# Pack attention and FFN on one core: the first batch's second softmax by halves of the tokens, two loads from ScalarE's queue, one subtraction on GpSimd, and new steps

## The chip, the cores and the metric

The program runs on 1 core of one Trainium2 chip. The metric is the device time in microseconds. Several executions were timed; one more was recorded by the hardware profiler, and all lines called profile come from it. In the lines PE is TensorE, PEld its weight loads, DVE is VectorE, ACT is ScalarE, POOL is GpSimd, and SP is the engine whose queue starts most transfers.

## The reference

Two attention stages with few "pack" tokens, then a feed-forward network. Per batch (8) and head (8): 576 tokens, head dimension 64, 32 pack tokens.

```python
def sm_attn(qq, kk, vv):
    s = scale * np.matmul(qq, kk.transpose(0, 1, 3, 2))
    s = s - np.max(s, axis=-1, keepdims=True)
    a = np.exp(s)
    a = a / (np.sum(a, axis=-1, keepdims=True) + 1e-09)
    return np.matmul(a, vv)
p_packed = sm_attn(p, k, v)          # first softmax: over 576 tokens
out = sm_attn(q, p_packed, p_packed) # second softmax: over 32 pack tokens
...                                  # heads side by side: x is 4608 x 512
h = x @ w_in                         # 512 x 2048
g = np.maximum(h, 0.0) + alpha * np.minimum(h, 0.0)
return g @ w_out                     # 2048 x 512
```

The weights w_in and w_out come as 64-bit floats and are turned into 32-bit ones on the chip.

## The kernel before

**Attention** is a Python generator, `attention(b, tp, exact)`, one for each batch and each half of its heads (tp 0 or 1: four heads, as two pairs). Between two `yield`s it issues one step: loads of K, the scores of the pack tokens (`scores`), their softmax, the transposed weights `aT` (L328, L332), the packed values (`pack`, L345 and L355, then L373), then the scores of all tokens against the packed keys and the **second softmax**. That one is laid out by 32-wide groups: a transpose of 32x32 blocks (L422 or L427, to `t`), a maximum of each group of 32 (L429, `m`), a subtraction (L431), an exponential on ScalarE (L433), a sum (L435, `z`), EPS added (L436), a reciprocal (L437), a product (L438), and a transpose back (L443, to `a_f`, in batch 0). Batches 0 and 1 use plain 32-bit matmuls (`exact`); the others split every operand in a high and a low part, so that `split_x`, `split_v` and `split_pw` have ScalarE cast the high part and VectorE or GpSimd subtract it (L180, L309, L455, L613). The low part of p, `s`, is such a subtraction (L256), done twice for each of the batches 2 to 7. For batch 0 the matmuls' scores stay in PSUM.

**The packed weights.** The packed values are multiplied into w_in first (`pw`), so that one FFN unit is `second softmax weights x pw`. `convert` makes a 32-bit tile of w_in or w_out from a 64-bit one (`wraw`): ScalarE makes `mag` and `low` (L121, L123), VectorE does L125, L128, L132 and L137 or L139, and for a split tile L141 and L142. Until it is needed for w_out, the space of the tiles of w_out holds raw tiles; `SPARE` says how many of them serve raw w_in tiles in turn. `packed_w_fine` (L525) and `packed_w_first` (L485) make pw for batch 0 from columns of w_in; `packed_w` (L595 to L597, copied out by L600) serves the other batches, from fresh, whole or split tiles. The split tiles are kept in DRAM (`w_split`) and loaded again (L567) for the batches 2 to 7.

**FFN units.** `first(k, f)` is a unit: the 288 tokens of half batch k by 128 of the 2048 hidden columns (`ps_h`: L625 in batch 0, L637 to L639 later), then the leaky ReLU: `neg` on ScalarE (L643), L644 on VectorE, the high part `gh` on ScalarE (L649), the low part `gl` on VectorE (L650). `second(k, f)` multiplies it by w_out into four accumulators (`acc`: L667 to L669), two units later (`AHEAD = 2`). A batch's columns are taken in sweeps, and the accumulators of a part are kept in `part`. At the end of a half batch four tiles `ot` go to DRAM (`outT`, L685).

**What sets the order.** Up to the first unit a string, `zzzAzzzzzPzzzoPzzzzozzzP`, says which generator takes its next step: z both attentions of batch 0, the second three steps behind the first, P `packed_w_fine`, o a w_out tile, A alpha. After that a list `plan` of (first unit, generator, pace) does: pace 1 is a step at each unit, 3 one at every third, -3 three at each. The numbers in it are `WO` (w_out: start, how many at once, then how many units apart), `AT1` (attention of batch 1), `PW1` (packed_w of batch 1 alone), `PW01` and `PW01B` (packed_w of batches 0 and 1), `A2` (attention of batches 2 and 3, their packed_w) and `AG` (the same for each later pair of batches). From the program so written, the framework's scheduler sets the order on each engine, by its own estimate of times, and places the semaphore waits. Each engine then takes its instructions strictly in order, and so does each engine's queue of transfers.

Of the kernel before, what the change touches and what calls it, by code (L numbers as in the profile page):

```python
# [28 lines left out]
def pack_attention_ffn_kernel(  # L29
# [199 lines left out]
    def attention(b, tp, exact=False):  # L229
# [11 lines left out]
        split = (lambda x: x) if exact else split_x  # L241
        if tp == 0:
            praw = sm.tile([P, NP, N], F32, name="praw", tag="praw", bufs=1)
            nc.sync.dma_start(out=praw, in_=pT[b])
        k0 = load_x(kT, b, pr0)
        k1 = load_x(kT, b, pr1)
        yield
        if tp == 0:
            for r in range(2):
                rs, cs = slice(r * 64, r * 64 + 64), slice(r * N, r * N + N)  # L250
                if exact:
                    for i in range(2):
                        nc.scalar.copy(out=s1f[rs, i::2, i, cs], in_=praw[rs, i::2])
                else:
                    nc.scalar.copy(out=s1[rs, :, 0, cs], in_=praw[rs])
                    nc.vector.tensor_tensor(  # L256
                        out=s1[rs, :, 1, cs], in0=praw[rs], in1=fv(s1[rs, :, 0, cs]),
                        op=ALU.subtract,
                    )
# [160 lines left out]
        if b == 0:  # L420
            for hf in range(2):
                nc.vector.transpose(  # L422
                    out=t1.rearrange("p g n -> p (g n)")[:, hf * HS : hf * HS + HS],
                    in_=s2[hf][:, :HS],
                )
# [3 lines left out]
        nc.vector.tensor_reduce(out=m2, in_=t1, axis=AX.X, op=ALU.max)  # L429
# [7 lines left out]
        nc.vector.reciprocal(out=z2, in_=z2)  # L437
        eng.tensor_tensor(out=t1, in0=t1, in1=z2.broadcast_to([P, NG, 32]), op=ALU.mult)  # L438
        yield
        if b < XF:  # L440
            if b not in result:
                result[b] = at.tile([P, 2, S], F32, name="a_f", tag="a_h")
            nc.vector.transpose(  # L443
                out=result[b][:, tp, :], in_=t1.rearrange("p g n -> p (g n)")
            )
            done.add(("a", b, tp))
            yield
            split_pt()
            return
# [4 lines left out]
        nc.scalar.copy(out=a_h[:, tp, :], in_=s2)
        nc.gpsimd.tensor_tensor(out=a_l[:, tp, :], in0=s2, in1=fv(a_h[:, tp, :]), op=ALU.subtract)  # L455
# [159 lines left out]

    def first(k, f):
        tok = slice((k % 2) * HS, (k % 2) * HS + HS)
        assert all(("a", k // 2, tp) in done for tp in range(2)), ("a", k)
        assert k < 2 and ("wf", f) in done or all(("w", k // 2, f // 4, pr) in done for pr in range(4)), ("w", k, f)
        ps = ps_h.tile([P, 512], F32, name="ps_h", tag="h")  # L620
        if k < 2 * XF:
            th, a_f = pw[k // 2, f // 4], result[k // 2]
            fs = slice((f % 4) * P, (f % 4) * P + P)
            for i in range(2):
                nc.tensor.matmul(  # L625
                    ps[:, :HS], th[:, i, fs], a_f[:, i, tok], start=(i == 0), stop=(i == 1)
                )
        else:
            a_h, a_l = result[k // 2]
            key = (k, f // 2)  # L630
            if key not in pj:
                split_pw(*key)
            th, tl = pj[key]
            fs = slice((f % 2) * P, (f % 2) * P + P)
            for i in range(2):
                hi, lo = (i == 0), (i == 1)
                nc.tensor.matmul(ps[:, :HS], th[:, i, fs], a_h[:, i, tok], start=hi, stop=False)  # L637
                nc.tensor.matmul(ps[:, :HS], th[:, i, fs], a_l[:, i, tok], start=False, stop=False)  # L638
                nc.tensor.matmul(ps[:, :HS], tl[:, i, fs], a_h[:, i, tok], start=False, stop=lo)  # L639
# [9 lines left out]
        nc.scalar.copy(out=gh, in_=x)  # L649
        nc.vector.tensor_tensor(out=gl, in0=x, in1=fv(gh), op=ALU.subtract)  # L650
        gs[k, f] = (gh, gl)
# [75 lines left out]

    def zipped(*gens):
        gens = list(gens)
        while gens:  # L730
            for x in list(gens):
                try:
                    next(x)
                except StopIteration:
                    gens.remove(x)
            yield

    def load_alpha():
        nc.sync.dma_start(out=al, in_=alpha)
        nc.vector.tensor_scalar(  # L740
            out=nal, in0=al, scalar1=-1.0, scalar2=1.0, op0=ALU.mult, op1=ALU.add
        )
        yield
# [5 lines left out]
    z = zipped(attention(0, 0, True), after(3, attention(0, 1, True)))  # L749
# [2 lines left out]
    la = load_alpha()

    for ch in "zzzAzzzzzPzzzoPzzzzozzzP":
        next({"z": z, "P": wf, "o": wo, "A": la}[ch], None)
# [3 lines left out]
    WO, W1, AT1 = (-7, 5, 4), 0, (-2, 2, -3)
    PW1, PW01, PW01B = (7, -2), (13, 3), (25, -8)  # L760
    A2 = (24, 29, 34, 38, 52)
    AG = (0, 4, 10, 17, 27)
# [58 lines left out]
```

## Time and profile before

| | |
|---|---|
| times of 3 runs | 806.47, 807.29 (median), 808.75 us |
| the profiled execution | 805.65 us |
| its span, first to last instruction | 803.9 us |
| mean granted TensorE clock | 0.991 of full speed |
| busy: TensorE, VectorE, ScalarE, GpSimd | 769.7, 500.7, 544.9, 305.6 us |
| moved by transfers | 93.79 MB |

The profiled execution's own time is 1.75 us above its span; that lies around the span. Most questions are asked of a stretch: which engine has no gap in it, and for whom TensorE waits. In rows of the timeline the first two numbers are start and duration in us, x the number of instructions merged in the row, and the bracket is the idle time of that engine before the row, with the instruction that ended it.

### The profile page before, as it was taken

The numbers are of one execution on the slowest core, as the hardware profiler recorded it, in microseconds if no ns is written. First come the engines' busy times: TensorE is split into PE (matmuls) and PEld (weight loads), VectorE is DVE, ScalarE is ACT, GpSimd is POOL, SyncE is SP. The second block draws the span as 40 slices with busy tenths as digits, with TensorE's granted clock in tenths as the row PEclk, the third lists the DMA queues.
The fourth block names the chain that finished last, engine by engine and source line by source line (L and its number), as shares of the span: only waits on it lengthen the run. The fifth ranks groups of instructions, "written<-read, shape, count | busy, mean of one in ns | idle before, by whom it ended". The sixth has DMA issues, their size and how long they took to land.

```text
span 803.9 us, 15166 instructions
## 1 busy us (share of the span) xinstructions
PE 769.7 (96%) x5376; PEld 729.5 (91%) x5376; DVE 500.7 (62%) x1110; ACT 544.9 (68%) x1258; POOL 305.6 (38%) x291
## 2 busy tenths in 40 slices
PE   5789999999989899999999999999999999999997
PEld 4557778989989799999999999999999999999997
DVE  4999899877877445666755265665753344444443
ACT  5787898876756877776768866776758744444443
POOL 2101311235436434666565135576443123222220
PEclk9989999999999999999999999999999999999999
DMA  9977777322223843222125722221007300000000
GB/s 299 379 246 240 254 283 255 118 67 70 89 77 94 274 162 107 84 60 89 53 71 172 240 97 61 74 60 61 1 31 228 113 30 2 30 1 31 1 31 30
DMA packets 58459, 93.79 MB, mean 117 GB/s; under 512 B 5136, under 2 KB 36880, under 8 KB 58384
## 3 DMA queue, kind: packets, MB, share of 16 engines
q1 hardware_dynamic: 58384, 92.83, 35.8%
q8 instruction: 42, 0.69, 0.3%
q14 instruction: 33, 0.27, 0.1%
HBM read 72.88 MB, written 19.92 MB: 115 GB/s over the span
## 4 chain that ended last, share of the span: by engine, by line
PE 83%; DVE 6%; ACT 3%; DMA 2%; issue 1%; SPq 0%; ACTq 0%; DVEq 0%
PE acc L667 16%; PE acc L669 16%; PE acc L668 15%; PE ps_h L637 7%; PE ps_h L638 7%; PE ps_h L639 7%; PE ps_h L625 3%; PE ps_m L350 2%; PE ps_m L595 2%; PE ps_m L216 2%; PE ps_m L597 1%; PE ps_m L596 1%; PE ps_m L217 1%; PE ps_m L328 1%; PE ps_m L212 1%
## 5 line engine op out<-in xcount | busy, mean ns | idle before, releaser
L667 PE MATMUL acc<-gh,wo 128*128 128x288 f32 x1024 | 286.1, 299 | 6.8 <-ACT gh L649 6.4
L668 PE MATMUL acc<-gh,wo 128*128 128x288 f32 x1024 | 282.6, 295 | 0.0
L644 DVE SCALAR_TENSOR_TENSOR ps_h<-neg,nal,ps_h 128x288 f32<-128x288 f32 x256 | 132.6, 518 | 146.8 <-ACT neg L643 146.1
L613 POOL TENSOR_TENSOR pwl<-pw,pwh 128x512 fp32r<-128x512 f32 x96 | 124.1, 1293 | 217.9 <-ACT pwh L611 183.2
L667 PEld LDWEIGHTS acc<-gh,wo 128*128 128x128 f32 x1024 | 192.7, 188 | 11.9 <-ACT gh L649 9.3
L669 PE MATMUL acc<-gl,wo 128*128 128x288 f32 x1024 | 201.5, 299 | 0.0
L668 PEld LDWEIGHTS acc<-gh,wo 128*128 128x128 f32 x1024 | 192.7, 188 | 1.5 <-issue 0.2
L650 DVE TENSOR_TENSOR gl<-ps_h,gh 128x288 fp32r<-128x288 f32 x256 | 116.0, 454 | 77.2 <-ACT gh L649 73.0
L669 PEld LDWEIGHTS acc<-gl,wo 128*128 128x128 f32 x1024 | 158.3, 188 | 2.8
L649 ACT CAST gh<-ps_h 128x288 fp32r<-128x288 f32 x256 | 102.0, 399 | 81.8 <-DVE ps_h L644 79.8
L637 PE MATMUL ps_h<-a_h,pwh 128*128 128x288 f32 x448 | 133.6, 298 | 3.4 <-DVE gl L650 3.4
L643 ACT ACTIVATE neg<-ps_h 128x288 f32<-128x288 f32 x256 | 104.6, 409 | 44.5 <-PE ps_h L639 33.8
L638 PE MATMUL ps_h<-a_l,pwh 128*128 128x288 f32 x448 | 132.1, 295 | 0.0
L639 PE MATMUL ps_h<-a_h,pwl 128*128 128x288 f32 x448 | 132.0, 295 | 0.0
L611 ACT CAST pwh<-pw 128x512 fp32r<-128x512 f32 x112 | 69.4, 620 | 61.9 <-PE ps_h L638 60.5
L180 POOL TENSOR_TENSOR xl<-xraw,xh 128x576 fp32r<-128x576 f32 x48 | 70.0, 1460 | 103.3 <-ACT xh L179 100.5
L637 PEld LDWEIGHTS ps_h<-a_h,pwh 128*128 128x128 f32 x448 | 84.2, 188 | 5.1 <-DVE gl L650 4.6
L638 PEld LDWEIGHTS ps_h<-a_l,pwh 128*128 128x128 f32 x448 | 84.3, 188 | 0.4
L639 PEld LDWEIGHTS ps_h<-a_h,pwl 128*128 128x128 f32 x448 | 84.1, 188 | 0.2
L600 ACT COPY pw<-ps_m 64x512 f32<-64x512 f32 x120 | 69.6, 580 | 7.2 <-PE ps_m L597 4.8
L309 POOL TENSOR_TENSOR vs<-vraw,vs 128x640 fp32r<-128x640 f32 x24 | 38.2, 1591 | 19.1 <-ACT vs L308 18.1
L219 ACT COPY lo<-ps_m 64x288 f32<-64x288 f32 x96 | 37.5, 396 | 6.5 <-PE ps_m L217 4.5
(128 smaller groups left out, 989.1 us busy)
## 6 DMA issues: line engine op xcount, KB each, us to landing
w<-w_split SPq DMA_DIRECT2D x48, 512.0 KB, 4.3
xraw<-in_kT SPq DMA_DIRECT2D x32, 288.0 KB, 2.9
xraw<-in_qT SPq DMA_DIRECT2D x32, 288.0 KB, 2.8
outT<-ot SPq DMA_DIRECT2D x64, 144.0 KB, 2.0
vraw<-in_v SPq DMA_DIRECT2D x32, 256.0 KB, 2.9
wraw<-in_w_in SPq DMA_DIRECT2D x16, 512.0 KB, 5.4
wraw<-in_w_out SPq DMA_DIRECT2D x16, 512.0 KB, 4.9
w_split<-w SPq DMA_DIRECT2D x16, 512.0 KB, 3.6
```

The lines of the kernel that those rows point to most:

```text
L180: nc.gpsimd.tensor_tensor(out=xl, in0=raw, in1=fv(xh), op=ALU.subtract)
L613: low.tensor_tensor(out=tl, in0=src, in1=fv(th), op=ALU.subtract)
L637: nc.tensor.matmul(ps[:, :HS], th[:, i, fs], a_h[:, i, tok], start=hi, stop=False)
L638: nc.tensor.matmul(ps[:, :HS], th[:, i, fs], a_l[:, i, tok], start=False, stop=False)
L639: nc.tensor.matmul(ps[:, :HS], tl[:, i, fs], a_h[:, i, tok], start=False, stop=lo)
L643: nc.scalar.activation(out=neg, in_=x, func=AF.Relu, scale=-1.0)
L644: nc.vector.scalar_tensor_tensor(out=x, in0=neg, scalar=nal[:, f : f + 1], in1=x, op0=ALU.mult, op1=ALU.add)
L649: nc.scalar.copy(out=gh, in_=x)
L650: nc.vector.tensor_tensor(out=gl, in0=x, in1=fv(gh), op=ALU.subtract)
L667: nc.tensor.matmul(acc[o][:, :HS], wo_t[f][:, 0, os_], gh, start=begin, stop=False)
L668: nc.tensor.matmul(acc[o][:, :HS], wo_t[f][:, 1, os_], gh, start=False, stop=False)
L669: nc.tensor.matmul(acc[o][:, :HS], wo_t[f][:, 0, os_], gl, start=False, stop=end)
```

## The change

1. **Second softmax of batch 0 in two halves of 288 tokens.** A generator `half(hf)` does the nine steps for 9 of the 18 groups of a partition, all of it on VectorE but the exponential. Each attention of batch 0 runs `half(0)` itself, and puts `half(1)` in the list `later`, which the plan steps twice at each unit from unit 0 on. A unit `first(k, f)` of batch 0 now needs only the half of its own 288 tokens.
2. **Loads.** p of batch 0 and alpha are issued from ScalarE's queue, alpha ahead of everything else; the first step of batch 0's attention is issued before ScalarE's first exponential.
3. **The subtraction L256** (low part of p, batches 2 to 7) goes from VectorE to GpSimd.
4. **Steps.** The string loses A and one z (`drain` takes what is left); SPARE is 4, not 6; WO, AT1, PW1, PW01B, A2 and AG have new numbers.

```diff
-    SPARE = 6
+    SPARE = 4
...
-            nc.sync.dma_start(out=praw, in_=pT[b])
+            (nc.scalar if b == 0 else nc.sync).dma_start(out=praw, in_=pT[b])
...
-                    nc.vector.tensor_tensor(
+                    nc.gpsimd.tensor_tensor(
                         out=s1[rs, :, 1, cs], in0=praw[rs], in1=fv(s1[rs, :, 0, cs]),
                         op=ALU.subtract,
                     )
...
+            def half(hf):
+                gs_ = slice(hf * (NG // 2), (hf + 1) * (NG // 2))
+                th, mh, zh = t1[:, gs_], m2[:, gs_], z2[:, gs_]
+                cols = slice(hf * HS, hf * HS + HS)
+                flat = th.rearrange("p g n -> p (g n)")
+                nc.vector.transpose(out=flat, in_=s2[hf][:, :HS])
+                nc.vector.tensor_reduce(out=mh, in_=th, axis=AX.X, op=ALU.max)
+                nc.vector.tensor_tensor(
+                    out=th, in0=th, in1=mh.broadcast_to([P, NG // 2, 32]), op=ALU.subtract
+                )
+                yield
+                nc.scalar.activation(out=th, in_=th, func=AF.Exp, scale=SCALE)
+                nc.vector.tensor_reduce(out=zh, in_=th, axis=AX.X, op=ALU.add)
+                nc.vector.tensor_scalar(out=zh, in0=zh, scalar1=EPS, scalar2=None, op0=ALU.add)
+                nc.vector.reciprocal(out=zh, in_=zh)
+                nc.vector.tensor_tensor(
+                    out=th, in0=th, in1=zh.broadcast_to([P, NG // 2, 32]), op=ALU.mult
+                )
+                yield
+                nc.vector.transpose(out=result[b][:, tp, cols], in_=flat)
+                done.add(("a", 2 * b + hf, tp))
+                yield
+
+            later.append(half(1))
+            yield from half(0)
+            split_pt()
+            return
...
-    def load_alpha():
-        nc.sync.dma_start(out=al, in_=alpha)
...
+    nc.scalar.dma_start(out=al, in_=alpha)
...
+    z = zipped(attention(0, 0, True), after(3, attention(0, 1, True)))
+    next(z)
...
-    for ch in "zzzAzzzzzPzzzoPzzzzozzzP":
+    for ch in "zzzzzzzzPzzzoPzzozzzzP":
...
-    WO, W1, AT1 = (-7, 5, 4), 0, (-2, 2, -3)
-    PW1, PW01, PW01B = (7, -2), (13, 3), (25, -8)
-    A2 = (24, 29, 34, 38, 52)
-    AG = (0, 4, 10, 17, 27)
+    WO, W1, AT1 = (-4, 5, 4), 0, (-1, 2, -6)
+    PW1, PW01, PW01B = (10, -2), (13, 3), (24, -8)
+    A2 = (24, 28, 35, 38, 52)
+    AG = (0, 4, 11, 17, 26)
...
+    plan += [(0, gen, -2) for gen in later]
```

Line numbers behind the change are 14 or 15 higher: L540, L500, L640, L659, L665 and L682 to L684 are the former L525, L485, L625, L644, L650 and L667 to L669; the halves' softmax stands in L431 to L445, with `t_318` for tp=0 and `t_348` for tp=1.

How the scheduler's order moves, first at the first FFN units. TensorE before (a row is one or more equal instructions; a 32-bit matmul is two in the trace):

```order
L525 MATMUL ps_m<-w_391,pt_103 128x128 x4
L625 MATMUL ps_h<-a_f,pw 128x288 x2
L485 MATMUL ps_m<-w_403,pt_103 128x512
L328 MATMUL ps_m<-ident,s_t 128x128 x3
L485 MATMUL ps_m<-w_454,pt_103 128x512
L328 MATMUL ps_m<-ident,s_t 128x128 x2
L625 MATMUL ps_h<-a_f,pw 128x288 x2
L667 MATMUL acc_579<-gh,wo_248 128x288
```

and now:

```order
L640 MATMUL ps_h<-a_f,pw 128x288 x2
L540 MATMUL ps_m<-w_361,pt_103 128x128 x4
L328 MATMUL ps_m<-ident,s_t 128x128 x5
L345 MATMUL ps_m<-vraw,aT 128x128 x10
L373 MATMUL ps_m<-ident,c 128x64
L640 MATMUL ps_h<-a_f,pw 128x288 x2
L373 MATMUL ps_m<-ident,c 128x64
L540 MATMUL ps_m<-w_389,pt_103 128x128 x4
L500 MATMUL ps_m<-w_401,pt_103 128x512
L500 MATMUL ps_m<-w_488,pt_103 128x512
L212 MATMUL ps_m<-xraw,ptf 64x288
L682 MATMUL acc_668<-gh,wo_267 128x288
```

The first L625 pair of two units (tp=0) and the second (tp=1) stood around three steps of other work; now the whole first pack of batch 1 (L328, L345, one L373) stands between them, and the products with w_in stand behind the second pair, ahead of the first accumulation.

VectorE at the same place, up to the end of the second softmax of tp=1, before:

```order
L137 ISA w_454<-mag,low 128x1024
L437 RECIPROCAL z_375<-z_375 128x18
L125 TENSOR_SCALAR mag<-mag 128x512
L299 TENSOR_SCALAR den<-den 128x1
L438 TENSOR_TENSOR t_349<-t_349,z_375 128x576
L128 TENSOR_SCALAR mag<-mag 128x512
L142 TENSOR_TENSOR wo_441<-mag,wo_441 128x512
L300 RECIPROCAL den<-den 128x1
L443 STREAM_TRANSPOSE a_f<-t_349 128x576
```

and now:

```order
L440 RECIPROCAL z_350<-z_350 128x9 x2
L142 TENSOR_TENSOR wo_449<-mag,wo_449 128x512
L300 RECIPROCAL den<-den 128x1
L132 SCALAR_TENSOR_TENSOR mag<-wraw_532,mag 128x512
L441 TENSOR_TENSOR t_348<-t_348,z_350 128x288 x2
L125 TENSOR_SCALAR mag<-mag 128x512
L139 ISA mag<-mag,low 128x1024
L445 STREAM_TRANSPOSE a_f<-t_348 128x288
L125 TENSOR_SCALAR mag<-mag 128x512
L445 STREAM_TRANSPOSE a_f<-t_348 128x288
```

The last transposes of tp=1 (to `a_f`) stand one behind the other, with one L125 between them, where one full one stood; the sums and products of both halves stand together ahead of them (x2). The softmax of tp=0, in halves, is through before.

The third place is SP's queue when packed_w of batches 2 and 3 loads its split tiles, at the end of batch 1's second half. Before:

```order
L173 DMA xraw<-in_qT 128x576 x2
L567 DMA w<-w_split 128x1024 x5
L685 DMA outT<-ot 128x288 x2
L567 DMA w<-w_split 128x1024
L685 DMA outT<-ot 128x288
L567 DMA w<-w_split 128x1024
```

and now:

```order
L173 DMA xraw<-in_qT 128x576 x2
L582 DMA w<-w_split 128x1024 x9
L700 DMA outT<-ot 128x288 x3
L582 DMA w<-w_split 128x1024
L700 DMA outT<-ot 128x288
L582 DMA w<-w_split 128x1024 x4
```

Five loads stood ahead of the outputs and the sixth behind two of them; now nine stand ahead.

More of the change, by code (lines that the diff above doesn't have):

```diff
@@ L419, in attention @@
         t1 = wk.tile([P, NG, 32], F32, name="t1", tag="w")
[L420 to L424, printed above, removed]
-                )
-        else:
-            nc.vector.transpose(out=t1.rearrange("p g n -> p (g n)"), in_=s2)
+        if b < XF:
+            if b not in result:
+                result[b] = at.tile([P, 2, S], F32, name="a_f", tag="a_h")
+            m2 = sm.tile([P, NG, 1], F32, name="m2", tag="m2")
+            z2 = sm.tile([P, NG, 1], F32, name="z2", tag="z2")
+            def half(hf):
[7 more added lines that the diff above has]
+                    out=th, in0=th, in1=mh.broadcast_to([P, NG // 2, 32]), op=ALU.subtract
+                )
+                yield
[14 more added lines that the diff above has]
+            return
@@ L428, in attention @@
+        nc.vector.transpose(out=t1.rearrange("p g n -> p (g n)"), in_=s2)
         m2 = sm.tile([P, NG, 1], F32, name="m2", tag="m2")
         nc.vector.tensor_reduce(out=m2, in_=t1, axis=AX.X, op=ALU.max)
-        eng = nc.vector if b < 1 else nc.gpsimd
-        eng.tensor_tensor(out=t1, in0=t1, in1=m2.broadcast_to([P, NG, 32]), op=ALU.subtract)
+        nc.gpsimd.tensor_tensor(out=t1, in0=t1, in1=m2.broadcast_to([P, NG, 32]), op=ALU.subtract)
         yield
@@ L437, in attention @@
         nc.vector.reciprocal(out=z2, in_=z2)
-        eng.tensor_tensor(out=t1, in0=t1, in1=z2.broadcast_to([P, NG, 32]), op=ALU.mult)
+        nc.gpsimd.tensor_tensor(out=t1, in0=t1, in1=z2.broadcast_to([P, NG, 32]), op=ALU.mult)
         yield
[L440 to L449, printed above, removed]
         if b not in result:
@@ L455, in attention @@
         nc.gpsimd.tensor_tensor(out=a_l[:, tp, :], in0=s2, in1=fv(a_h[:, tp, :]), op=ALU.subtract)
-        done.add(("a", b, tp))
+        done.update(("a", 2 * b + hf, tp) for hf in range(2))
         yield
@@ L617, in first @@
         tok = slice((k % 2) * HS, (k % 2) * HS + HS)
-        assert all(("a", k // 2, tp) in done for tp in range(2)), ("a", k)
+        assert all(("a", k, tp) in done for tp in range(2)), ("a", k)
         assert k < 2 and ("wf", f) in done or all(("w", k // 2, f // 4, pr) in done for pr in range(4)), ("w", k, f)
@@ L689, in pack_attention_ffn_kernel @@
     done, owner = set(), {}
+    later = []
     SWEEPS = [(0, 4, 8, 12), (0, 8)] + [(0,)] * (B - 2)
@@ L736, in zipped @@
             yield
-    def load_alpha():
[L739 to L743, printed above, removed]
+    nc.scalar.dma_start(out=al, in_=alpha)
+    nc.vector.tensor_scalar(
+        out=nal, in0=al, scalar1=-1.0, scalar2=1.0, op0=ALU.mult, op1=ALU.add
+    )
+    z = zipped(attention(0, 0, True), after(3, attention(0, 1, True)))
+    next(z)
     first_exp = sm.tile([P, 1], F32, name="first_exp", tag="den")
@@ L747, in pack_attention_ffn_kernel @@
     nc.scalar.activation(out=first_exp, in_=first_exp, func=AF.Exp)
[L749 removed]
     wf = packed_w_fine(0)
     wo = w_out_steps(range(NF))
[L752 to L755 removed]
+    for ch in "zzzzzzzzPzzzoPzzozzzzP":
+        next({"z": z, "P": wf, "o": wo}[ch], None)
     drain(z)
[L759 to L762 removed]
+    WO, W1, AT1 = (-4, 5, 4), 0, (-1, 2, -6)
+    PW1, PW01, PW01B = (10, -2), (13, 3), (24, -8)
+    A2 = (24, 28, 35, 38, 52)
+    AG = (0, 4, 11, 17, 26)
     plan = [(0, wf, 1), (WO[0], slower(WO[1], WO[2], wo), 1), (W1, packed_w_first(1), 1)]
+    plan += [(0, gen, -2) for gen in later]
     plan += [(AT1[0], attention(1, 0, True), AT1[2]), (AT1[1], attention(1, 1, True), AT1[2])]
```

## The prediction

> **What bounds the kernel now.** I read the engine totals first, then the TensorE waits, then one-microsecond stretches around each wait, and last what stood on the engine waited for.
>
> ```profile
> PE 769.7 (96%) x5376; PEld 729.5 (91%) x5376; DVE 500.7 (62%) x1110; ACT 544.9 (68%) x1258; POOL 305.6 (38%) x291
> PE 83%; DVE 6%; ACT 3%; DMA 2%; issue 1%; SPq 0%; ACTq 0%; DVEq 0%
> ```
>
> TensorE is the bound: 34.2 us of the 803.9 us span are idle. The change removes no matmul, so it can win only from idle time and from the slower clock behind it. The longest waits, in the order of the program (the bracket gives the wait before the row and its releaser):
>
> ```profile
> 4.49 7.16 PE L207 MATMUL acc<-xraw,s1f 128*128 128x288 f32 x16 [4.49 <-POOL vraw L188]
> 38.37 2.29 PE L625 MATMUL ps_h<-a_f,pw 128*128 128x288 f32 x4 [2.40 <-DVE a_f L443]
> 49.34 0.40 PE L667 MATMUL acc<-gh,wo 128*128 128x288 f32 x1 [2.45 <-ACT gh L649]
> 51.43 1.93 PE L485 MATMUL ps_m<-w,pt 128*128 128x512 f32 x2 [0.76 <-DVE w L137]
> 117.17 0.40 PE L667 MATMUL acc<-gh,wo 128*128 128x288 f32 x1 [1.31 <-ACT gh L649]
> 228.16 0.40 PE L637 MATMUL ps_h<-a_h,pwh 128*128 128x288 f32 x1 [2.05 <-DVE gl L650]
> 273.98 0.47 PE L595 MATMUL ps_m<-w,pt 128*128 128x512 f32 x1 [0.60 <-DMA w<-w_split]
> 278.38 0.47 PE L595 MATMUL ps_m<-w,pt 128*128 128x512 f32 x1 [1.71 <-DMA w<-w_split]
> 397.18 0.40 PE L667 MATMUL acc<-gh,wo 128*128 128x288 f32 x1 [1.21 <-ACT gh L649]
> 498.80 0.40 PE L637 MATMUL ps_h<-a_h,pwh 128*128 128x288 f32 x1 [0.40 <-DVE gl L650]
> ```
>
> Next, stretches (busy time of PE, PEld, DVE, ACT, POOL, then clock, DMA share, GB/s; the first row is of DVE alone, the 229 to 233 row of PE alone):
>
> ```profile
> 20.00:60.00 40.00, 39.91 (x87) 0.87 0.90 312
> 35.00:40.00 5.00, 2.60 (x12) 1.95 (x11) 4.97 (x11) 1.66 (x5) 0.00 (x0) 0.80 1.02 377
> 40.00:45.00 5.00, 4.72 (x9) 1.53 (x7) 4.97 (x15) 4.17 (x9) 0.00 (x0) 0.52 0.90 277
> 50.00:60.00 10.00, 9.24 (x42) 6.80 (x41) 10.00 (x23) 7.67 (x16) 0.20 (x1) 0.83 0.80 259
> 100.00:120.00 20.00, 18.60 (x109) 15.20 (x108) 19.55 (x41) 18.67 (x39) 3.00 (x2) 1.00 0.76 275
> 229.00:233.00 4.00, 4.00 (x21) 0.57 0.28 78
> ```
>
> VectorE has no gap from 20 to 60 us: there its order decides when anything arrives. And a TensorE wait costs twice: behind the waits of 2.40 and 2.05 us the granted clock fell to about half, 0.52 at 40 to 45 us and 0.57 at 229 to 233 us.
>
> **Part 1: second softmax by halves.** What it is made of:
>
> ```profile
> L125 DVE TENSOR_SCALAR mag<-mag 128x512 f32<-128x512 f32 x13 | 5.2, 403 | 0.0
> L422 DVE STREAM_TRANSPOSE t<-acc 128x288 f32<-128x288 f32 x4 | 1.9, 468 | 0.0
> 23.83 0.74 DVE L429 TENSOR_REDUCE m<-t 128x18 f32<-128x576 f32 x1
> 24.50 0.68 DVE L132 SCALAR_TENSOR_TENSOR mag<-wraw,mag 128x512 uint32<-128x512 uint32 x1
> 33.17 0.25 DVE L437 RECIPROCAL z<-z 128x18 f32<-128x18 f32 x1
> 44.84 0.76 DVE L443 STREAM_TRANSPOSE a_f<-t 128x576 f32<-128x576 f32 x1
> ```
>
> Successive instructions overlap: a 576-wide reduce starts 0.67 us before the next instruction (23.83 to 24.50), so 0.67 is its cost, 0.07 below its own duration. By the same step a 288-wide one costs about 0.40 (the transpose's 468 ns less 0.07) or 0.37 for a reduce; I take 0.375. The conversion's L125 costs 403 ns less 0.07, 0.33, and L132, and L139 like it, 0.60. Eight wide operations of 0.67 (maximum, subtraction, sum, product, of two pair groups) become sixteen of 0.375: +0.64 us. Two more reciprocals of 0.18 and two more small additions, less than that: about +0.5 with room. The last transpose, twice 0.68, becomes four times 0.40: +0.24. VectorE gets about 1.4 us more; the pair of L256, which leaves it, gives 0.6 back: net +0.8.
>
> Is the first half early? Of tp=0, yes. Of tp=1, without which no unit ends, hardly: the new order puts it behind both halves of tp=0. I count from the same start, the conversion at 17.06. Ahead of it VectorE now also does one L125, one L132 and one L139 more (0.33+0.60+0.60), no L256 (-0.60), and softmax work +0.64, +0.5 and +0.12 (two transposes of 0.40 for one of 0.68): +2.2 us. It starts near 47.0, not 44.84, and the first FFN unit ends later. What differs is the cover. Before, TensorE waited 2.45 and 0.76 us for gh and a converted w. Now L540 on w_389 (eight instructions), L500 on w_401 and on w_488 and an L212 stand behind the first units: 1.2 and twice 1.1 us, by
>
> ```profile
> 34.81 1.16 PE L525 MATMUL ps_m<-w,pt 128*128 128x128 f32 x8
> 59.55 1.12 PE L485 MATMUL ps_m<-w,pt 128*128 128x512 f32 x2
> ```
>
> and about half a microsecond for the L212: some 3.8 us of work, so this gap closes. A gap opens earlier: batch 1's L328 stands ahead of the second pair, and needs an exponential whose maximum (L280, L281) ends on VectorE near 41, so TensorE idles from about 37 to 42. Idle before: 2.40+2.45+0.76 = 5.6; now about 5. Clock before: at most 1.0+2.4+1.7 = 5.1 lost (length times missing share of the three windows); now one slow stretch instead of two, about 3 to 5. Gain between -2 (if the pack of batch 1 runs at half speed right up to 49 and pushes the units) and +3; I take **+1.0**, nearer the low end, since the longer gap is the surer one.
>
> The +0.8 us of VectorE work: hidden where it waits for TensorE; from 100 to 120 us it is busy 19.55 of 20 us and TensorE waits for it (1.31 at 117), so I charge it whole, **-0.8** (0 to -1.7).
>
> **Part 2: loads from ScalarE's queue.** Alpha's issue on SP, one of the two that leave it, and the first wait for w_in:
>
> ```profile
> 2.12 0.43 SPq L739 DMA_DIRECT2D al<-in_alpha  x1
> 12.83 0.66 ACT L121 ACTIVATE mag<-wraw 128x512 f32<-128x512 f32 x1 [2.19 <-DMA wraw<-in_w_in]
> ```
>
> K goes out 0.4 to 0.9 us sooner, so the 4.49 may become 4.1. On ScalarE two issues now stand ahead of the table load and the first copies of p; ScalarE was idle long after those. But the next thing that VectorE needs is w_in at 12.83, and one more Q load now stands ahead of it on SP. I take 0 (-0.4 to +0.9).
>
> **Part 3: L256 from VectorE to POOL.** Six pairs, of batches 2 to 7. Three cost 0.60 us, three did not:
>
> ```profile
> 39.47 0.60 DVE L256 TENSOR_TENSOR s<-praw,s 64x128 fp32r<-64x128 f32 x2
> 225.24 1.83 DVE L256 TENSOR_TENSOR s<-praw,s 64x128 fp32r<-64x128 f32 x2
> 393.32 2.17 DVE L256 TENSOR_TENSOR s<-praw,s 64x128 fp32r<-64x128 f32 x2
> 496.17 1.43 DVE L256 TENSOR_TENSOR s<-praw,s 64x128 fp32r<-64x128 f32 x2
> 225.51 1.41 POOL L455 TENSOR_TENSOR a_l<-s,a_h 128x576 fp32r<-128x576 f32 x1 [1.84 <-ACT a_h L454]
> 394.05 1.29 POOL L613 TENSOR_TENSOR pwl<-pw,pwh 128x512 fp32r<-128x512 f32 x1 [0.15 <-ACT pwh L611]
> L393 POOL TENSOR_TENSOR pt<-ptf,pt 128x128 fp32r<-128x128 f32 x2 | 0.9, 452 | 0.1
> ```
>
> Each long pair ends within about 0.2 us of the end of a POOL subtraction that overlaps it (227.07 against 226.92, 395.49 against 395.34). Behind it wait L644, gh, gl, and TensorE: 2.05 us at 228, 1.21 at 397, 0.40 at 498. Gone with it: 1.83 of the 2.05, the slow clock behind it (4 us by 0.43 missing, 1.7, of which I count 1.65), 1.21 and 0.40: **+5.1**, at most 5.3, at least 0. POOL, 38% busy, takes 12 subtractions; its nearest row is 452 ns for 128x128 (L393), so some 1 us a batch, beside a subtraction of 1.4 us on the way to the same scores. Hidden by POOL's idle time; if not, up to 1 us a batch.
>
> The Trainium skill (Perfetto Trace Analysis, Optimizing Scalar/DVE Operations) speaks against this: the two engines share an SBUF read port, so moving work between them might not help. The rows above agree with the shared port. By that rule the sum would lose this term; my reason against it is that after batch 1's units no other VectorE instruction here reads two SBUF tiles.
>
> **Part 4: the steps.** The two issues on SP around the load that delayed TensorE at 278, the load in the chain, and the median time to landing of the w_in loads:
>
> ```profile
> 272.28 0.81 SPq L685 DMA_DIRECT2D outT<-ot  x2
> 273.20 0.41 SPq L567 DMA_DIRECT2D w<-w_split  x1
> 273.20 5.04 DMA w<-w_split
> wraw<-in_w_in SPq DMA_DIRECT2D x16, 512.0 KB, 5.4
> ```
>
> That load stood behind two outputs which waited for VectorE; it landed at 273.20+5.04 = 278.24. In the new order nine, not five, w_split loads stand ahead of these outputs: the 0.60+1.71 = 2.3 us go. In the last group it is the reverse: a load now stands between outputs, with packing one step earlier (AG 26). Same kind of wait, with a quarter of the price: -0.5. Together **+1.8** (0 to 2.3). SPARE 4 leaves fewer buffers for w_in at first; landing takes 5.4 us, and three conversions of some 2.5 us lie between reuses. Zero.
>
> **Sum.** +1.0 -0.8 +5.1 +1.8 = 7.1 us. The profiled execution took 805.65, so 798.6 there; it lies 1.6 below the median of 807.29, against which the time is to be read: **800.2**.
>
> **Rivals.** (a) L256 only trades places: POOL's pair holds up POOL's subtractions or VectorE's, and TensorE waits as long elsewhere. For it: half the pairs did collide. Against: the place moves off the chain to gl. Gain 2.0, 805.3; the rule of the Trainium skill named in part 3 would give this. (b) The start gets worse: the clock stays low through two windows after the long gap and VectorE's later tp=1 is not covered; -3 instead of +1, 804.2. (c) The start and 100 to 140 us gain too: w_out steps begin later (WO -4), which frees a w_in buffer when batch 0/1's packing converts, so the 1.31 at 117 goes, and as much of the slow clock at the start: 2.6 more, 797.6. (d) Slower: POOL takes its instructions in order, and L256 there waits for ScalarE's cast of p; behind it stand the subtractions (L613) of every unit. POOL's idle ahead of an L613 is 183.2 us over 96, 1.9 each, so a wait below 1.9 is hidden; it decides from about 3.7 us a batch: at five late batches 5 x (3.7-1.9) = 9.0, 809.2 or more. Against: ahead of none of the six pairs on VectorE does the trace show idle time, so the cast was there.
>
> ```profile
> L613 POOL TENSOR_TENSOR pwl<-pw,pwh 128x512 fp32r<-128x512 f32 x96 | 124.1, 1293 | 217.9 <-ACT pwh L611 183.2 <-PE acc L669 15.6 <-PE ps_h L639 11.7
> ```
>
> **Chances.** Forecast 0.45, (a) 0.15, (b) 0.17, (c) 0.14, (d) 0.09. What a measurement can tell is 0.3%, 2.4 us: faster below 804.9, slower above 809.7. (a) counts as same, (d) as slower, the others as faster: 0.76, 0.15, 0.09. The range runs from below (c) to above (a), leaving out (d) and the ends: 796.5 to 806.0; with all low ends met it would pass 806.
>
> **What would show it.** Right: no VectorE L256, no wait over 0.5 us for gl at the places of 228 and 397, clock 1.00 there; no wait of packing for w_split in the first group; TensorE idle once, near 37 to 42, then filled to the first accumulation at 52 to 54. Wrong: clock at 0.5 through 50 us; waits for POOL's s or xl; VectorE's softmax rows above 0.45 us for a half; new waits of over 2 us after 60 us.

## The result, and the profile after

The changed kernel takes 800.37 us (median of 4 runs, 800.3 to 802.3), the kernel before 806.88 in the same comparison: ratio 0.9922, 95% interval 0.9899 to 0.9945. The forecast was 800.2. The profiled execution took 800.34 us, with a span of 798.5. Its totals and its chain by engine:

```profile
PE 766.9 (96%) x5376; PEld 729.6 (91%) x5376; DVE 501.1 (63%) x1112; ACT 542.7 (68%) x1260; POOL 312.4 (39%) x303
PE 78%; DVE 2%; ACT 1%; DMA 1%; issue 0%; ACTq 0%; DVEq 0%
```

TensorE is idle for 31.6 us instead of 34.2, and busy 2.8 us less. So the span fell by 5.4 us, and half of that is not idle time but matmuls that ran faster or overlapped more. Where the waits went shows in stretches (busy time of PE, PEld, DVE, ACT, POOL, then clock, DMA share, GB/s). Before:

```profile
0.00:60.00 60.00, 43.17 (x191) 30.35 (x192) 48.09 (x113) 40.88 (x99) 9.12 (x28) 0.91 0.90 308
60.00:180.00 120.00, 113.61 (x714) 97.78 (x713) 105.49 (x220) 101.39 (x232) 28.79 (x29) 1.00 0.61 204
220.00:240.00 20.00, 17.78 (x124) 17.44 (x123) 15.65 (x35) 11.95 (x31) 6.98 (x9) 0.91 0.29 89
380.00:400.00 20.00, 18.80 (x143) 18.56 (x141) 13.34 (x29) 13.64 (x33) 9.85 (x9) 1.00 0.20 53
```

and after:

```profile
0.00:60.00 60.00, 43.83 (x211) 33.40 (x212) 48.47 (x125) 41.22 (x105) 12.83 (x33) 0.91 0.89 294
60.00:180.00 120.00, 109.96 (x681) 93.85 (x680) 107.25 (x214) 101.56 (x229) 30.62 (x31) 1.00 0.64 214
220.00:240.00 20.00, 20.00 (x155) 19.84 (x154) 13.81 (x34) 13.53 (x35) 7.65 (x11) 1.00 0.34 97
380.00:400.00 20.00, 20.00 (x155) 20.00 (x154) 14.44 (x34) 14.87 (x37) 11.88 (x11) 1.00 0.22 64
```

The two late stretches, where L256 had collided with GpSimd, have no idle time left, and the clock at 220 to 240 us is whole. The first 60 us gained 0.7 us (43.83 less 43.17 busy). From 60 to 180 us TensorE lost 3.7. The waits of TensorE after the change that the argument turns on (start, duration, in brackets the wait ahead and its releaser):

```profile
6.10 4.18 PE L207 MATMUL acc<-xraw,s1f 128*128 128x288 f32 x8 [6.10 <-ACT s1f L253]
41.23 1.17 PE L328 MATMUL ps_m<-ident,s_t 128*128 128x128 f32 x5 [3.12 <-ACT s_t L294]
124.79 0.40 PE L682 MATMUL acc<-gh,wo 128*128 128x288 f32 x1 [1.08 <-ACT gh L664]
131.29 0.51 PE L610 MATMUL ps_m<-w,pt 128*128 128x512 f32 x1 [0.96 <-ACT w L141]
135.42 0.40 PE L652 MATMUL ps_h<-a_h,pwh 128*128 128x288 f32 x1 [0.82 <-DVE gl L665]
141.49 0.40 PE L682 MATMUL acc<-gh,wo 128*128 128x288 f32 x1 [1.56 <-ACT gh L664]
149.33 0.74 PE L328 MATMUL ps_m<-ident,s_t 128*128 128x128 f32 x5 [1.83 <-DVE s_t L302]
279.03 0.47 PE L610 MATMUL ps_m<-w,pt 128*128 128x512 f32 x1 [0.59 <-DMA w<-w_split]
```

No wait over 0.5 us stands at the places of 228, 397 and 498. There is one long gap near 41 us, as forecast (3.12 us, and 1.15 close behind it). Between 124 and 150 us stands a row of waits of 0.8 to 1.8 us, 6.25 in sum; in the kernel before the waits over 0.5 us from 115 to 150 were 1.31 at 117, 0.80 at 126 and 0.66 at 148. The waits for `w_split` fell from 0.60 + 1.71 to 0.59.

### The profile page after: what moved, and what is told of

Same layout as the page of the kernel before. It is cut to its first block, busy times and chain, and to the rows that moved or that the text cites. A ratio compares the mean times of both kernels' runs of the same rounds, so it can differ in the third digit from the quotient of the medians.

```text
span 798.5 us, 15192 instructions
## 1 busy us (share of the span) xinstructions
PE 766.9 (96%) x5376; PEld 729.6 (91%) x5376; DVE 501.1 (63%) x1112; ACT 542.7 (68%) x1260; POOL 312.4 (39%) x303
## 4 chain that ended last, share of the span: by engine, by line
PE 78%; DVE 2%; ACT 1%; DMA 1%; issue 0%; ACTq 0%; DVEq 0%
PE acc L682 15%; PE acc L683 15%; PE acc L684 15%; PE ps_h L652 7%; PE ps_h L653 7%; PE ps_h L654 7%; PE ps_h L640 2%; PE ps_m L350 2%; PE ps_m L216 1%; PE ps_m L217 1%; PE ps_m L610 1%; PE ps_m L612 1%; PE ps_m L611 1%; PE ps_m L328 1%; DMA w<-w_split 1%; PE ps_m L375 0%
## 5 line engine op out<-in xcount | busy, mean ns | idle before, releaser
L682 PE MATMUL acc<-gh,wo 128*128 128x288 f32 x1024 | 287.2, 300 | 3.7 <-ACT gh L664 3.7
L659 DVE SCALAR_TENSOR_TENSOR ps_h<-neg,nal,ps_h 128x288 f32<-128x288 f32 x256 | 132.0, 517 | 141.0 <-ACT neg L658 140.1
L628 POOL TENSOR_TENSOR pwl<-pw,pwh 128x512 fp32r<-128x512 f32 x96 | 124.3, 1295 | 213.4 <-ACT pwh L626 192.1
L684 PE MATMUL acc<-gl,wo 128*128 128x288 f32 x1024 | 202.3, 300 | 0.0
L682 PEld LDWEIGHTS acc<-gh,wo 128*128 128x128 f32 x1024 | 192.3, 188 | 9.7 <-ACT gh L664 6.5
L665 DVE TENSOR_TENSOR gl<-ps_h,gh 128x288 fp32r<-128x288 f32 x256 | 115.8, 454 | 81.1 <-ACT gh L664 78.6
L684 PEld LDWEIGHTS acc<-gl,wo 128*128 128x128 f32 x1024 | 158.4, 188 | 4.2 <-issue 0.9
L180 POOL TENSOR_TENSOR xl<-xraw,xh 128x576 fp32r<-128x576 f32 x48 | 69.0, 1440 | 93.0 <-ACT xh L179 88.8
```

The source lines that it names most:

```text
L628: low.tensor_tensor(out=tl, in0=src, in1=fv(th), op=ALU.subtract)
L659: nc.vector.scalar_tensor_tensor(out=x, in0=neg, scalar=nal[:, f : f + 1], in1=x, op0=ALU.mult, op1=ALU.add)
L682: nc.tensor.matmul(acc[o][:, :HS], wo_t[f][:, 0, os_], gh, start=begin, stop=False)
L684: nc.tensor.matmul(acc[o][:, :HS], wo_t[f][:, 0, os_], gl, start=False, stop=end)
```

## The experiments

### Four single edits, order left free

The first four kernels each undo or do one part in the source and let the scheduler set the order anew.

```diff
 b_l256: the kernel before
-                    nc.vector.tensor_tensor(out=s1[rs, :, 1, cs], ...
+                    nc.gpsimd.tensor_tensor(out=s1[rs, :, 1, cs], ...
 a_l256v: the changed kernel
-                    nc.gpsimd.tensor_tensor(out=s1[rs, :, 1, cs], ...
+                    nc.vector.tensor_tensor(out=s1[rs, :, 1, cs], ...
 a_praw_sp: the changed kernel
-            (nc.scalar if b == 0 else nc.sync).dma_start(out=praw, in_=pT[b])
+            nc.sync.dma_start(out=praw, in_=pT[b])
 a_p_first: the changed kernel
     next(z)
+    nc.scalar.dma_start(out=al, in_=alpha)
```

(In a_p_first alpha's load and the step that makes `nal` move behind `next(z)`.)

> The kernel before with one edit: the subtraction L256 on GpSimd, not on VectorE (batches 2 to 7). Theory: the three collisions were the cause of the TensorE waits at 228, 397 and 498 us; the waits for gl and gh there fall below 0.5 us, the granted clock in the stretch of 229 to 233 us is 1.00, and the time falls by 4.5 to 5.3 us against before (to about 801.8). Rival: the work only trades places on a shared port; GpSimd's pair holds up the subtractions L455 or L613, TensorE waits 1 to 2 us at the same places, and the time falls by less than 2.4 us.

> The changed kernel with L256 back on VectorE, nothing else edited (the scheduler may move some rows). Theory: the collisions of VectorE's pair with GpSimd's subtractions come back where L256 meets them, in two to four of the six batches, with TensorE waits of 0.4 to 2 us behind them: slower than the changed kernel by 2 to 6 us (802.5 to 806.5). Rival, that the gain came from the new steps around L256 and not from its engine: within 1 us of the changed kernel, 800.4.

> The changed kernel with p of batch 0 issued from SyncE's queue again, alpha alone on ScalarE's. Theory: p landed 4.1 us after its issue on ScalarE's queue and put off TensorE's first matmul to 6.10 us; from SyncE's queue it lands by 3 to 3.5 us, the first matmul starts at 4.1 to 4.9 us, and the first accumulation (L682) comes 1 to 1.6 us sooner than 52.87: faster by 0.8 to 1.6 us (799.2). Rival: the later start is hidden, since VectorE has no gap from 20 us on and its first conversion waits for w_in: the first matmul sooner, the first accumulation where it was, within 0.4 us (800.4).

> The changed kernel with p issued first on ScalarE's queue and alpha behind it. Theory one, that alpha ahead of it costs p only its issue: p issued at 0.74 instead of 1.18 us, lands at 4.9 instead of 5.3, first matmul 0.4 us sooner, time less by 0 to 0.4 us. Theory two, that p shares the transfer engines with the first loads of K on SyncE's queue and lands late because of them: p ahead of these loads lands by 3.5 us, the first matmul starts by 4.5 us. Rival: the time to landing belongs to ScalarE's queue, 4.1 us again, and nothing beyond the 0.4 us changes.

| kernel | us | ratio to before, 95% interval |
|---|---|---|
| b_l256 | 809.69 | 1.0022, 1.0004 to 1.0040 |
| a_l256v | 817.73 | 1.0135, 1.0114 to 1.0156 |
| a_praw_sp | 815.75 | 1.0111, 1.0092 to 1.0129 |
| a_p_first | 814.92 | 1.0101, 1.0083 to 1.0119 |

None came out where any theory put it. Turning two small loads round can hardly cost 14 us by itself: these runs measure another order of everything. In a_l256v three of TensorE's longest waits were for things that L256 does not touch (releaser, total, times, longest):

```profile
PE ps_m L328 <- ACT s_t L294: 4.2, 1, 4.2
PE ps_m L610 <- ACT w L141: 3.5, 1, 3.5
PE ps_m L610 <- DMA w<-w_split: 2.0, 1, 2.0
```

They settle nothing on the parts of the change, except that in a_p_first p still took 3.6 us to land on ScalarE's queue (4.1 in the changed kernel; 1.9 on SyncE's queue, in the kernel before and in a_praw_sp).

### The order held

So all later kernels keep the recorded order of the kernel they start from. From each instruction to the one that stood ahead of it on its engine goes an edge that orders the two and waits for nothing. Only instructions that an edit adds or moves are left to the scheduler. No kernel holds the order and changes nothing else; but h_b_split and h_half below stay at the time of before (0.9986 and 1.0017), and h_a_praw and h_a_order at that of the changed kernel, so the edges themselves seem to cost little.

```diff
+def hold_order(tc):
+    ins = list(tc.nc.cur_bb.bb.instructions)
+    info = mybir.DependencyInfo(mybir.DependencyClass.NoSync, mybir.DependencyReason.DATA)
+    for prev, k in recorded_neighbours:      # of each engine, from a table
+        tc.add_manual_dep(ins[k], ins[prev].name, info, reason="hold_order")
```

**L256 alone**, in both directions: h_b_l256 is the edit of b_l256 and h_a_l256v that of a_l256v, each with the order held.

> The kernel before with L256 on GpSimd, and every other instruction of every engine held in its order of before by edges that wait for nothing; only where GpSimd takes the twelve L256 is left to the scheduler. Theory: the collisions were the cause, the waits for gl and gh at 228, 397 and 498 us and the slow clock behind the first go, 4.5 to 5.3 us off (801.9). Rival one, it only trades places: the waits stay or move to GpSimd's subtractions, less than 2.4 us off. Rival two, what the first run of this edit showed with the order left free (0.2 per cent slower) is the edit's own worth: no gain with the order held either.

> The changed kernel with L256 on VectorE, everything else held in the changed kernel's order. Theory: a pair costs 0.6 us where GpSimd subtracts nothing beside it and 1.4 to 2.2 us where it does; VectorE is late by so much at two or three of the six places and TensorE waits: slower than the changed kernel by 1 to 5 us (801.4 to 805.4). Rival: in this order the pairs meet no subtraction of GpSimd, and the time stays within 0.8 us of 800.4.

h_b_l256 took 801.61 us, before 807.54: ratio 0.9920, 0.9896 to 0.9945. That is as much as the whole change gains, from one line. Its stretches and its pairs on GpSimd, at the places that cost most before:

```profile
220.00:240.00 20.00, 19.77 (x150) 19.43 (x150) 16.69 (x39) 14.61 (x37) 9.34 (x12) 1.00 0.32 93
380.00:400.00 20.00, 20.00 (x155) 20.00 (x154) 14.68 (x33) 15.53 (x37) 12.09 (x11) 1.00 0.23 63
223.69 0.98 POOL L256 TENSOR_TENSOR s<-praw,s 64x128 fp32r<-64x128 f32 x2
390.77 1.01 POOL L256 TENSOR_TENSOR s<-praw,s 64x128 fp32r<-64x128 f32 x2
```

h_a_l256v took 803.42 us, ratio to before 0.9959, 0.9941 to 0.9976: some 3 us worse than the changed kernel (the two intervals just touch), and 2 us worse than the two other kernels held in that order (h_a_praw, h_a_order). Its pairs on VectorE took 0.72 to 1.52 us instead of 0.60. The longest, what ran on GpSimd, and the stretch at 220:

```profile
387.20 1.42 POOL L180 TENSOR_TENSOR xl<-xraw,xh 128x576 fp32r<-128x576 f32 x1
387.57 1.52 DVE L256 TENSOR_TENSOR s<-praw,s 64x128 fp32r<-64x128 f32 x2
220.00:240.00 20.00, 19.88 (x150) 19.27 (x149) 14.79 (x37) 12.69 (x33) 7.49 (x10) 1.00 0.32 93
```

So the trade-places rival is out. How much a pair costs on VectorE depends on what it happens to meet. And this kernel, which has every part of the change but L256, is still 3 to 4 us faster than before (medians 4.1, ratio 3.3): in the new order the pair behind the longest wait (2.05 us at 228 before) took 1.20 us at 219.96, TensorE hardly waited behind it, and the clock stayed whole. So L256 is worth some 6 us in the old order and 2 to 3 in the new one; the parts of the change do not add up.

**p from SyncE's queue**: a_praw_sp with the order held.

> The changed kernel with p of batch 0 issued first on SyncE's queue, everything else held in order. Theory: TensorE's first matmul comes at 4.1 to 4.9 instead of 6.10 us and the first accumulation (L682) 0.8 to 1.6 us sooner than 52.87: faster than the changed kernel by 0.8 to 1.6 us (799.2). Rival: the start is hidden behind the first w_in load and VectorE, the first matmul is sooner and the first accumulation is not: within 0.5 us of 800.4.

801.39 us, ratio to before 0.9929, 0.9906 to 0.9951: not told from the changed kernel. TensorE started 1.4 us sooner, waited 1.1 us longer at 41, and the first accumulation came at 52.67, only 0.2 us sooner:

```profile
4.70 5.54 PE L207 MATMUL acc<-xraw,s1f 128*128 128x288 f32 x12 [4.70 <-DMA xraw<-in_kT]
41.73 1.33 PE L328 MATMUL ps_m<-ident,s_t 128*128 128x128 f32 x5 [4.17 <-ACT s_t L294]
```

The rival holds: most of the start is hidden.

**Nine loads of `w_split` ahead of the outputs**, in the kernel before; only SyncE's queue differs.

```diff
-w x5, outT x2, w, outT, w, outT, w, w, ...
+w x9, outT x4, w, ...
```

> The kernel before with one change in SyncE's queue: nine, not five, loads of w_split stand ahead of the four outputs of batch 1's second half; everything else held in order. Theory: the load that delayed TensorE at 278 us no longer stands behind outputs that wait for VectorE; the waits of 0.60 and 1.71 us there go, 1.8 to 2.3 us off (804.8). Rival: the loads then wait for their buffers instead, and the outputs behind them; TensorE waits as long, within 0.8 us of 806.9.

805.92 us against 807.54, ratio 0.9986, 0.9968 to 1.0005: the interval holds no change as well as the 1.8 us that I had summed. The rows speak against the theory. The two waits (2.31 us in sum) became one for the same load and one for `gh` (2.58 in sum):

```profile
276.85 0.47 PE L595 MATMUL ps_m<-w,pt 128*128 128x512 f32 x1 [1.49 <-DMA w<-w_split]
281.42 0.40 PE L667 MATMUL acc<-gh,wo 128*128 128x288 f32 x1 [1.09 <-ACT gh L649]
```

**The halves alone**, in the order of before.

```diff
-            if b == 0: ... the nine steps on 18 groups ...
+            later.append(half(1))
+            yield from half(0)
...
+    plan += [(0, gen, -2) for gen in later]
```

> The kernel before with the first part of the change alone: the second softmax of batch 0 by halves, everything else (loads, L256, steps) as before and held in the order of before; only the split instructions are placed by the scheduler. Theory: the halves by themselves buy nothing, since the units stand where they stood and both pair groups are needed; VectorE's 1.4 us more falls in the stretch without a gap, and the first accumulation comes 0.5 to 1.5 us later than 49.34: 0 to 1.5 us slower than before (807.5). Rival: the first half's transposes come earlier than the whole ones, the wait of 2.40 us for a_f at 38 shrinks by a microsecond or more with the slow clock behind it, and the time falls by 1 to 3 us.

807.70 us against 806.90, ratio 1.0017, 0.9994 to 1.0039: nothing to gain and perhaps a little lost. In the profiled run the wait of 2.40 us for `a_f` at 38 is gone, but one of 3.35 on VectorE stands at 42, and the first accumulation came 1.3 us later than the 49.34 of before:

```profile
42.00 2.04 PE L500 MATMUL ps_m<-w,pt 128*128 128x512 f32 x2 [3.35 <-DVE z L439]
50.62 0.40 PE L682 MATMUL acc<-gh,wo 128*128 128x288 f32 x1 [2.70 <-ACT gh L664]
```

**More subtractions to GpSimd**: if one helps, do sixteen more? L142 of the w_out tiles, in the changed kernel and in h_b_l256.

```diff
-    def convert(src, raw, place, whole=None, room=None):
+    def convert(src, raw, place, whole=None, room=None, low_on=nc.vector):
...
-        nc.vector.tensor_tensor(out=lo, in0=mag, in1=fv(hi), op=ALU.subtract)
+        low_on.tensor_tensor(out=lo, in0=mag, in1=fv(hi), op=ALU.subtract)
...
-        return convert(w_out[f * P : (f + 1) * P, :], new_raw(f), place)
+        return convert(w_out[f * P : (f + 1) * P, :], new_raw(f), place, low_on=nc.gpsimd)
```

> The changed kernel with the low-part subtraction of the sixteen w_out tiles (L142, 0.68 us each) on GpSimd too, all else held in the changed kernel's order. Theory one, VectorE's work is what bounds 20 to 60 and 100 to 160 us: four or five of them leave the first stretch, four the second, the first accumulation comes 2 to 3 us sooner and TensorE's waits of 7 us between 120 and 150 shrink by 2: faster than the changed kernel by 2 to 5 us (797). Theory two, the collisions that made L256 dear on VectorE come back from the other side: the conversions that VectorE runs beside it (L125, L132, L139) read two tiles of SBUF or run at double rate, and are held up by as much as GpSimd's 1.3 us: no gain, 800 to 803.

> The kernel before with L256 and the sixteen L142 of w_out on GpSimd, all else held in the order of before. Beside the run with L256 alone (801.61): theory one, VectorE is the bound of the first 60 us and six subtractions leave it: 2 to 4 us faster than that, 798 to 799.5, which would be ahead of the changed kernel. Theory two, GpSimd's subtractions hold up the conversions beside them: 801 to 804.

803.08 us (ratio to before 0.9955, 0.9939 to 0.9971) and 804.42 (0.9967, 0.9950 to 0.9983): 2.7 and 2.8 us worse than without (the first two intervals just touch, the others don't). Groups of VectorE from 20 to 160 us, in the changed kernel:

```profile
L132 DVE SCALAR_TENSOR_TENSOR mag<-wraw,mag 128x512 uint32<-128x512 uint32 x27 | 18.7, 697 | 0.0
L128 DVE TENSOR_SCALAR mag<-mag 128x512 uint32<-128x512 uint32 x27 | 11.3, 419 | 0.0
L142 DVE TENSOR_TENSOR w<-mag,w 128x512 fp32r<-128x512 f32 x8 | 6.0, 755 | 0.0
L142 DVE TENSOR_TENSOR wo<-mag,wo 128x512 fp32r<-128x512 f32 x14 | 10.3, 738 | 1.2 <-ACT wo L141 1.0
```

and in h_a_wo, with GpSimd's fourteen:

```profile
L132 DVE SCALAR_TENSOR_TENSOR mag<-wraw,mag 128x512 uint32<-128x512 uint32 x27 | 21.1, 785 | 0.0
L128 DVE TENSOR_SCALAR mag<-mag 128x512 uint32<-128x512 uint32 x27 | 13.5, 504 | 0.0
L142 DVE TENSOR_TENSOR w<-mag,w 128x512 fp32r<-128x512 f32 x8 | 7.4, 923 | 0.0
L142 POOL TENSOR_TENSOR wo<-mag,wo 128x512 fp32r<-128x512 f32 x14 | 20.5, 1461 | 61.4 <-ACT wo L141 26.7 <-DMA wraw<-in_w_out 23.4 <-issue 11.2
```

10.3 us left VectorE, 6.0 came back in these three groups (2.4 + 2.2 + 1.4; L139 took 0.5 less, L125 and L137 the same), and the moved work takes twice as long where it is now. Here the work does trade places.

**Some rows moved by hand** in the changed kernel, between 37 and 50 us.

```diff
 VectorE
-L280, L137, L128, L132, L438 x2, L281, ...
+L280, L281, L137, L128, L132, L438 x2, ...
-L125, L128, L132, L139 of w_out tile 3 and two L125, ahead of L445 x2 of tp=1
+L445 x2 of tp=1, then these six
 ScalarE
-L121, L123, L294, L141, L123, L332 x2
+L294, L121, L123, L332 x2, L141, L123
-L141 of tile 3, L123, L121, ahead of L658 x2
+L658 x2, then L141 of tile 3, L123, L121
```

> The changed kernel with only the order of some rows between 37 and 50 us moved by hand. On VectorE L281 (the maximum that batch 1's first exponential waits for) directly behind its L280 instead of 2.2 us later, and the conversion of the fourth w_out tile with two more L125 behind the last transposes of the second softmax of tp=1 instead of ahead of them; on ScalarE the exponential L294 and the copies L332 ahead of the conversions they waited behind, and that tile's L141 with the two casts after it behind the first two L658. Everything else is held. Theory one, the wait of 3.12 us at 41 and the slow clock behind it are worth their time: L328 at about 39.5, the last transposes of tp=1 about 2 us sooner, the first accumulation at 49.5 to 51 instead of 52.87, and 2 to 4 us off (796.5 to 798.5), ahead of both kernels. Theory two, VectorE's work paces TensorE up to 150 us: the first accumulation comes sooner and the lead is given back as longer waits between 60 and 150; within 0.8 us of 800.4.

801.35 us, ratio to before 0.9917, 0.9890 to 0.9945: not told from the changed kernel. The last transposes of tp=1 came 2 to 3 us sooner (one row from 43.75, instead of 45.89 and 46.59) and the wait at 41 halved, but the first accumulation stayed at 52.84:

```profile
39.57 0.66 PE L328 MATMUL ps_m<-ident,s_t 128*128 128x128 f32 x4 [1.56 <-ACT s_t L294]
46.09 0.43 PE L373 MATMUL ps_m<-ident,c 128*128 128x64 f32 x2 [0.89 <-ACT c L355]
50.30 1.98 PE L500 MATMUL ps_m<-w,pt 128*128 128x512 f32 x4 [1.64 <-ACT ptf L382]
52.84 0.40 PE L682 MATMUL acc<-gh,wo 128*128 128x288 f32 x1
```

The wait moved from 41 to 50 us, to ScalarE's copy of `ptf`, which the three rows I had moved now stand ahead of. That is neither theory: theory one's lead was lost before 60 us, to my own edit, so the run cannot say whether VectorE would have taken it back later. It says only that the gap at 41 was not worth its length in this order. No kernel here beats the changed one.

## Why the prediction was right, and where it was not

**The time** was right, the terms less so. Against the profiled execution of before (805.65) I forecast 7.1 us and it was 5.3; the medians fell by 6.5. The profiled run of before lay 1.6 us below its median and the one after lies on it, and that 1.6, carried over as an offset, hid most of the miss. That the forecast of 800.2 came so near is luck.

**L256, +5.1: right, for the order of before.** With that order held it measures 5.9 us (0.9920, 0.9896 to 0.9945). In the rows of the changed kernel it is 2.2 us of idle time at 220 to 240 (2.0 in h_b_l256), 1.2 at 380 to 400, 0.4 behind, and, as an estimate, 0.09 of the clock over 20 us, 1.8: 5.6. The clock there is 0.91 in h_half and h_b_split too, which leave L256 on VectorE, and 1.00 in h_b_l256. GpSimd's pairs took about a microsecond, as counted; in the changed kernel nobody waited for them. The argument against the rule of the Trainium skill (Perfetto Trace Analysis, Optimizing Scalar/DVE Operations) holds, but it covers only half of the pairs: VectorE's last instruction with two full tiles in SBUF, L628 for batch 1's units, stands at 254.29 us, and three of the six pairs come before. What the rows show is that from 161 us on VectorE ran nothing beside a pair that took longer than elsewhere, as here:

```profile
386.54 0.74 DVE L280 TENSOR_REDUCE nmx<-s_t 128x1 f32<-128x576 f32 x1
386.94 0.98 POOL L256 TENSOR_TENSOR s<-praw,s 64x128 fp32r<-64x128 f32 x2
387.20 0.51 DVE L659 SCALAR_TENSOR_TENSOR ps_h<-neg,nal,ps_h 128x288 f32<-128x288 f32 x1
```

In the sixteen L142, beside which VectorE converts weights, the rule was right.

**Steps, +1.8: right in the row, not shown as a cause.** The row fell by 1.7 us (2.31 to 0.59), though one wait for `w_split` is left where I had said none. But the mechanism I named, nine loads ahead of the outputs, did not remove the waits by itself in the order of before (2.58 us). What else in the new order makes it hold there stays open.

**Start, +1.0: size right, cause not shown.** The stretch gained 0.7 us of idle time and the clock over it is the same 0.91. The gap at 41, the last transposes of tp=1 (45.89 and 46.59, forecast 47.0) and the first accumulation (52.87) came as forecast, and the clock did not stay low through 50 us (0.50 from 42 to 48, 0.93 from 48 to 50). The transposes of a half took up to 0.48 us, over the 0.45 that I had named as a sign of being wrong, but no longer than the 0.468 of such rows before. The halves by themselves gain nothing and bring the accumulation 1.3 us later, about what the extra VectorE work was put at; the 0.7 would then be the new order's. But 0.7 is less than two executions of nearly one order differ by: h_b_l256 was busy 41.47 us in this stretch, before 43.17, with the clock at 0.94 instead of 0.91 (last section).

**Loads, 0: right, by the wrong rows.** I expected TensorE's first wait at 4.1 us; it was 6.10, since p took 4.1 us on ScalarE's queue. I had hidden p behind w_in, and it was hidden, though behind the wait at 41.

**VectorE from 100 to 140, -0.8 (0 to -1.7): mis-sized, the one failed term.** TensorE lost 1.8 us in that stretch (37.00 to 35.24 busy) and another 1.8 from 140 to 180, where I had no term: -3.7 from 60 to 180 us. I priced the instructions added and not the order. The waits at 135, 141 and 149 return within 2 us of their places in h_a_l256v, h_a_praw, h_a_wo and h_a_order, whichever engine L256 or p is on: the second 1.56 us long in all four, the third 1.83 or 1.84. In the order of before the only wait near these two is one of 0.7 us at 148. One link of them shows: at 132.65 VectorE's L139 took 1.92 us, held by a subtraction of GpSimd (in the order of before the same meeting cost 1.12), and behind it wait L659, `gl` and TensorE at 135.42.

```profile
132.49 1.53 POOL L180 TENSOR_TENSOR xl<-xraw,xh 128x576 fp32r<-128x576 f32 x1 [26.06 <-ACT xh L179]
132.65 1.92 DVE L139 CUSTOM_DVE_ANT_0 mag<-mag,low 128x1024 uint16<-128x1024 uint16 x1
134.49 0.51 DVE L659 SCALAR_TENSOR_TENSOR ps_h<-neg,nal,ps_h 128x288 f32<-128x288 f32 x1
134.91 0.45 DVE L665 TENSOR_TENSOR gl<-ps_h,gh 128x288 fp32r<-128x288 f32 x1
```

Which step moved the rest (1.56 at 141, 1.83 at 149) was not settled: the steps were not tried one by one with the order held. Rival (c) had the wait of 1.31 us at 117 going, and it went; the others cost more.

By these rows the terms sum to 4.3 us (+0.7 -3.7 +5.6 +1.7) of the 5.3; the last microsecond lies in busy time that I have not placed. On top of L256 all the rest came to about nothing, 800.37 against 801.61 with L256 alone, intervals almost the same, where I had summed +2.0. But that does not make the rest worthless: without L256 it gives 3 to 4 us (h_a_l256v, 0.9959, 0.9941 to 0.9976). In that kernel the collision near 220 us no longer reaches TensorE, which is 2.1 us of idle time and, as an estimate, 1.8 of the clock. Moving L256 and the new order cure the same stretch, and it can be cured only once.

## What to carry to other kernels

Where a scheduler sets the order, an edit in the source measures the edit and a new order together: here edits worth 0 to 6 us moved the time by up to 17. Hold the recorded order and change one thing, and a single moved subtraction gives as much as the whole change. Then take the same thing out of the changed kernel too: here it was worth about half there, because the new order had already removed part of what it cures. And a price for a moved step is not only its instructions: read which two engines meet where it now stands.

## What the runs showed of the hardware that was not expected

GpSimd's TENSOR_TENSOR holds up more of VectorE than pairs of SBUF tiles: a TENSOR_SCALAR with one source, L125, took 1.77 us beside it, while 29 rows of it with GpSimd idle, in the first 300 us, average 0.42. L461, a TENSOR_SCALAR of 128x18, took 1.40 us at 207.02 beside L180 and 0.17 with GpSimd idle.

```profile
84.61 2.01 POOL L309 TENSOR_TENSOR vs<-vraw,vs 128x640 fp32r<-128x640 f32 x1
85.12 1.77 DVE L125 TENSOR_SCALAR mag<-mag 128x512 f32<-128x512 f32 x1
```

Instructions that read PSUM were not held: L665 averages 0.452 us in 34 rows of the first 300 us with GpSimd idle and 0.455 in 29 rows with it busy, L659 0.51 in both. The Trainium skill (SBUF — State Buffer, Who interferes with whom) describes an exclusive lock, for which instructions with two SBUF inputs and certain copies, casts and `tensor_scalar` contend; the rows here agree, though the trace does not say in which mode L125 and L461 ran.

A wait of TensorE did not fix when the slow clock came. In h_b_l256, whose instructions stand in the order of before but for L256, the same wait (2.39 us, at 38) was followed by a whole clock, and half the clock came from 48 on. Before, and then h_b_l256 (busy time of TensorE, then clock, DMA share, GB/s):

```profile
38.00:46.00 8.00, 7.10 (x14) 0.58 0.88 296
48.00:54.00 6.00, 3.90 (x15) 0.80 0.65 206
38.00:46.00 8.00, 4.98 (x17) 1.00 0.85 285
48.00:54.00 6.00, 5.38 (x17) 0.50 0.71 209
```

So the price of the slow clock in the first 60 us, which the prediction read from one execution, is not the same in the next one. Behind the wait at 228 to 232 it was: the clock of that stretch was 0.91 in all three profiled kernels that keep the order of before with L256 on VectorE.
